# Pooled attention and a top-1 expert layer in one kernel: one two-bank buffer for an attention product, and its division in single VectorE instructions

## The chip, the cores and the metric

The kernel runs on one core of a Trainium2 chip. The core has TensorE (PE in the profile, its weight loads PEld), VectorE (DVE), ScalarE (ACT), GpSimd (POOL) and a queue of DMA issues on SyncE (SP). The metric is the device time of one execution in microseconds; of several runs the median counts.

## The reference

Attention over keys and values that are averaged in groups of 8 rows, then a layer of 8 experts, of which each token takes the one with the largest gate logit. Batch 8, 8 heads, 576 positions, head width 64; so 4608 tokens of width 512, and experts of 512 x 1024 and 1024 x 512.

```python
def _attn_ref(q, k, v):
    k_p = k.reshape(B, H, Sp, pool, D).mean(axis=3)
    v_p = v.reshape(B, H, Sp, pool, D).mean(axis=3)
    scores = scale * np.matmul(q, k_p.transpose(0, 1, 3, 2))
    scores = scores - np.max(scores, axis=-1, keepdims=True)
    attn = np.exp(scores)
    attn = attn / (np.sum(attn, axis=-1, keepdims=True) + 1e-09)
    return np.matmul(attn, v_p).astype(np.float32)

def _moe_ref(x, modality_id, w_gate, modality_bias, w1, w2):
    logits = x @ w_gate + modality_bias[modality_id]
    e_idx = np.argmax(logits, axis=1)
    probs = softmax(logits)
    gate_w = probs[np.arange(N), e_idx]
    for e in range(E):
        mask = e_idx == e
        h = np.maximum(x[mask] @ w1[e], 0.0)
        out[mask] = gate_w[mask, None] * (h @ w2[e])
```

The softmax of the gate is shortened here; the attention's output, transposed to one row per token, is x.

## The kernel before

The order of all instructions on all engines is the order in which the program writes them; buffers come from pools, and a recording layer adds the waits. A wait is put where an instruction touches a buffer that another engine wrote or read, so which bytes count as one buffer decides who waits for whom.

**Attention.** The 4608 tokens are 36 tiles of 128. Two tiles, or one tile of two half-filled sequences ("mixed"), make a step; there are 20 steps, and the loop over n (lines 874 to 947) writes parts of three neighbouring steps between each other. For a tile the scores of all heads go through max, subtraction and exp (s_dve, s_act), are turned (t_pe, t_act), and multiplied by the averaged values (a_pe). Each head's values carry 73 columns: 64 values, 8 products with the gate's weights, and a 1 whose product is the softmax's sum. Eight heads times 73 columns need two PSUM banks of 512 columns: bank u holds heads 4u to 4u+3. In a_pe each bank is a tile of its own, av0 and av1, with one buffer each; three groups of matmuls fill each (lines 570 and 574, two of 570 and one of 574).

x_dve (lines 576 to 608) divides. For each of the two banks VectorE takes the four sums (L593), their reciprocals (L595), then writes the values into xb (L597) and the gate's products into lg (L599). Between them gap(1) lets one instruction out of a list of small fillers, `drip`: the routing of the tiles already done. These are the softmax over the gate's logits, the counts of tokens by expert (cum, L684) and the early table of slots. Some fillers are held until TensorE has a place for them. When four or five tiles are complete, their rows go to xs in DRAM (L607, SyncE).

GpSimd averages keys and values meanwhile (fold, L294 to L296), and splits the first expert's weights (split_lo, L139) into a rounded part and a rest.

**Expert layer.** Slots of 256 tokens with one expert each; 19 slots are run. A slot has eight blocks f of 128 hidden columns. `first` (lines 159 to 168) makes 12 matmuls into hp[f % 2], ScalarE writes the rounded hidden values hh (L165), VectorE the rest hlo (L167); `second` makes six matmuls of hh and hlo into op (L1100). They alternate: block f+1's first layer stands before block f's second layer, so that hh and hlo have time.

```python
hp = [ps_av.tile([P, 512], F32, tag=f"av{i}", name=f"hp{i}") for i in range(2)]
...
first(f, a, b, hp[f % 2][:, 0:SLOT], *(at or (hhs[f % 2], hlos[f % 2])))()
```

hp0 and hp1 take the banks of av0 and av1 over. The number of slots is known only at run time; the last slot's second half (`end`, lines 1158 to 1169) stands in a branch and orders the second layer differently: between two blocks stand three matmuls for one half of the tokens, and the other half's follow at the end.

Of the kernel before, what the change touches and what calls it, by code (L numbers as in the profile page):

```python
# [9 lines left out]
F32 = mybir.dt.float32  # L10
# [5 lines left out]
ALU = mybir.AluOpType  # L16
# [6 lines left out]
P = 128  # L23
# [7 lines left out]
def kernel(  # L31
# [12 lines left out]
    nc = tc.nc  # L44
    ctx.enter_context(tc.manual_schedule(engines=ENGINES))
    B, H, S, HD = q.shape
    NTOK, D = out.shape
    E, _, FF = w1.shape
    POOL = 8
# [3 lines left out]
    VC = HD + E + 1  # L53
# [15 lines left out]
    ps_av = ctx.enter_context(tc.tile_pool(name="ps_av", bufs=1, space=PSUM))  # L69
# [114 lines left out]
    with ExitStack() as actx:  # L184
        ap = actx.enter_context(tc.tile_pool(name="ap", bufs=1))
# [270 lines left out]
        def gap(n=2):  # L456

            for _ in range(n):
                if drip and drip[0] not in held:
                    drip.pop(0)()  # L460
# [7 lines left out]
        qts, pqs, scs, pes, pps, pts, avs, xb, lgs = {}, {}, {}, {}, {}, {}, {}, {}, {}  # L468
# [87 lines left out]
        def a_pe(t):  # L556
            n, z = tile_step[t]
            b, jj, _ = steps[n]
            pt, pt4 = pts.pop(t), pt4z[z]
            av = [ps_av.tile([P, 512], F32, tag=f"av{u}", name=f"av_{t}_{u}") for u in range(2)]  # L560
            avs[t] = av
            if jj is not None:
                halves = [(slice(0, P), b % NB)]
            else:
                halves = [(slice(64 * y, 64 * y + 64), (b - 1 + y) % NB) for y in range(2)]
            for u in range(2):
                for gg in range(2):
                    c = 2 * u + gg
                    for hs, y in halves:
                        nc.tensor.matmul(av[u][hs, 2 * VC * gg:2 * VC * (gg + 1)], pt[:, c, hs],  # L570
                                         vw[y][:, c].rearrange("p a x -> p (a x)"), start=(gg == 0), stop=False)
                dst4 = av[u][:, 0:4 * VC].rearrange("p (g x) -> p g x", g=2)[:, :, VC:2 * VC]
                for hs, y in halves:
                    nc.tensor.matmul(dst4[hs], pt4[:, hs], v4[y][:, 2 * u:2 * u + 2, :], start=False, stop=True)  # L574

        def x_dve(t):
            n, z = tile_step[t]
            g, gi = tile_group[t]
            av = avs.pop(t)
# [6 lines left out]
            if gi == 0:  # L586
                lgs[g] = ap.tile([P, GT, H, E], F32, tag="lg", bufs=2, name=f"lg_{g}")
            xo = xb[b, 4] if mixed else xb[b][:, gi % 5, :]
            for u in range(2):
                avv = av[u][:, 0:4 * VC].rearrange("p (h x) -> p h x", h=4)  # L590
                r = ap.tile([P, 4], F32, tag="r", bufs=4, name=f"r_{t}_{u}")
                rb = r.rearrange("p (h o) -> p h o", o=1)
                nc.vector.tensor_scalar(r, avv[:, :, VC - 1], float(POOL), 1e-9 * POOL, op0=ALU.mult, op1=ALU.add)  # L593
                gap(1)
                nc.vector.reciprocal(r, r)  # L595
                gap(1)
                nc.vector.tensor_tensor(xo[:, u * D // 2:(u + 1) * D // 2].rearrange("p (h d) -> p h d", h=4), avv[:, :, 0:HD],  # L597
                                        rb.to_broadcast([P, 4, HD]), op=ALU.mult)
                nc.vector.tensor_tensor(lgs[g][:, gi, 4 * u:4 * u + 4, :], avv[:, :, HD:HD + E],  # L599
                                        rb.to_broadcast([P, 4, E]), op=ALU.mult)  # L600

            if mixed:
                for z in range(2):
# [355 lines left out]
    xl.append(mp.tile([P, ND, SLOT], F32R, name="xl1"))  # L959
    ps_op = ctx.enter_context(tc.tile_pool(name="ps_op", bufs=1, space=PSUM))  # L960
    op = [[ps_op.tile([P, 512], F32, name=f"op{i}_{z}") for z in range(2)] for i in range(2)]
    hp = [ps_av.tile([P, 512], F32, tag=f"av{i}", name=f"hp{i}") for i in range(2)]
    hhs = [mp.tile([P, SLOT], F32R, name=f"hh{i}") for i in range(2)]
    hlos = [mp.tile([P, SLOT], F32R, name=f"hlo{i}") for i in range(2)]

# [263 lines left out]
```

## Time and profile before

| | us |
|---|---|
| median of 3 runs (662.88 to 668.61) | 663.94 |
| the profiled execution | 669.24 |
| its span, first to last instruction | 667.4 |

The profile is one execution, taken by the hardware profiler; times in its rows are from the span's start. "L597" is line 597 of the kernel, and `xb<-av,r` says that xb is written from av and r. "x72" counts instructions; a mean in ns belongs to one of them. A row of the waits names who waited, for whom, the sum in us, how often and the longest. A row of the timeline has start and duration in us, and in brackets how long the engine stood before and what released it. Matmuls are pipelined: they begin every 0.1 to 0.3 us, though each lasts some 0.3 to 0.4 in the rows.

Attention ends at about 210 us, the expert loop runs from about 222 to 640, and the last slot ends the kernel.

### The profile page before, as it was taken

The numbers are of one execution on the slowest core, as the hardware profiler recorded it, in microseconds if no ns is written. First come the engines' busy times: TensorE is split into PE (matmuls) and PEld (weight loads), VectorE is DVE, ScalarE is ACT, GpSimd is POOL, SyncE is SP. The second block draws the span as 40 slices with busy tenths as digits, with TensorE's granted clock in tenths as the row PEclk, the third lists the DMA queues.
The fourth block names the chain that finished last, engine by engine and source line by source line (L and its number), as shares of the span: only waits on it lengthen the run. The fifth ranks groups of instructions, "written<-read, shape, count | busy, mean of one in ns | idle before, by whom it ended". The sixth has DMA issues, their size and how long they took to land.

```text
span 667.4 us, 12673 instructions
## 1 busy us (share of the span) xinstructions
PE 613.7 (92%) x4313; PEld 556.7 (83%) x4313; DVE 433.9 (65%) x955; ACT 340.9 (51%) x625; POOL 211.6 (32%) x236
## 2 busy tenths in 40 slices
PE   4399899998599799999999999999999999999993
PEld 3289788887498699999999999999999999999982
DVE  4677789899975656766655656665565666556540
ACT  2347556676351254544555555555555555555530
POOL 5388673955801022112112112211211321131221
PEclk9799899999799899999999999999999999999998
DMA  9999999998232372011011055101105510110120
GB/s 244 223 363 241 316 155 232 274 172 243 53 80 64 87 230 64 18 48 64 12 54 63 20 179 182 50 17 61 63 18 178 186 38 16 63 65 17 48 69 15
DMA packets 65403, 76.54 MB, mean 115 GB/s; under 512 B 15407, under 2 KB 42031, under 8 KB 65328
## 3 DMA queue, kind: packets, MB, share of 16 engines
q1 hardware_dynamic: 59088, 55.68, 32.1%
q0 software_dynamic: 6240, 19.95, 9.0%
q8 instruction: 36, 0.59, 0.4%
q14 instruction: 39, 0.32, 0.2%
HBM read 119.64 MB, written 19.42 MB: 208 GB/s over the span
## 4 chain that ended last, share of the span: by engine, by line
PE 67%; DMA 17%; DVE 4%; SPq 4%; issue 3%; POOL 2%; ACT 1%; POOLq 0%; DVEq 0%; ACTq 0%
PE hp L163 27%; PE op L1100 26%; DMA out_dram<-ob,sidx 7%; DMA v<-in_v_dram 5%; PE av L570 3%; PE xt L154 2%; DMA q<-in_q_dram 2%; PE ph L163 2%; DMA xs<-xb 2%; DMA k<-in_k_dram 1%; PE av L574 1%; DVE sm L672 1%; PE pp L535 1%; PE sc L506 1%; PE ptab L1006 1%
## 5 line engine op out<-in xcount | busy, mean ns | idle before, releaser
L136 ACT CAST hl<-raw 128x1024 fp32r<-128x1024 f32 x138 | 145.0, 1051 | 143.8 <-PE op L1100 141.8
L163 PE MATMUL hp<-xh,hl 128*128 128x256 f32 x1152 | 186.0, 284 | 0.6 <-issue 0.6
L163 PEld LDWEIGHTS hp<-xh,hl 128*128 128x128 f32 x1152 | 166.1, 189 | 11.7 <-issue 1.0
L1100 PE MATMUL op<-hl,hh 128*128 128x512 f32 x556 | 174.2, 394 | 0.0
L1086 POOL DMA_INDIRECT out_dram<-ob,sidx x38 | 53.7, 1413 | 353.3 <-DVE ob L1082 268.4
L139 DVE TENSOR_TENSOR hl<-raw,hl 128x1024 fp32r<-128x1024 f32 x136 | 165.3, 1216 | 0.0
L167 DVE SCALAR_TENSOR_TENSOR hlo<-hp,hh 128x256 fp32r<-128x256 f32 x139 | 58.9, 424 | 140.5 <-ACT hh L165 129.7
L1100 PE MATMUL op<-hl,hlo 128*128 128x512 f32 x278 | 108.9, 392 | 0.0
L1100 PEld LDWEIGHTS op<-hl,hh 128*128 128x128 f32 x556 | 95.2, 189 | 12.3
L163 PE MATMUL hp<-xl,hl 128*128 128x256 f32 x576 | 92.0, 282 | 0.0
L163 PEld LDWEIGHTS hp<-xl,hl 128*128 128x128 f32 x576 | 78.9, 190 | 0.0
L165 ACT ACTIVATE hh<-hp 128x256 fp32r<-128x256 f32 x139 | 53.3, 383 | 49.3 <-PE hp L163 47.4
L1100 PEld LDWEIGHTS op<-hl,hlo 128*128 128x128 f32 x278 | 52.2, 188 | 11.8
L570 PE MATMUL av<-vw,pt 128*128 128x146 f32 (+1 forms) x320 | 52.1, 303 | 9.3 <-DVE lg L599 8.4
L570 PEld LDWEIGHTS av<-vw,pt 128*128 128x128 f32 (+1 forms) x320 | 41.3, 187 | 11.5 <-DVE lg L599 9.1
L143 POOL DMA_INDIRECT xg<-xs,gidx x40 | 42.9, 1074 | 12.1 <-issue 9.5
L506 PE MATMUL sc<-kt,qt 128*128 128x144 f32 x256 | 38.2, 293 | 0.8 <-DVE sb L516 0.6
L513 DVE TENSOR_REDUCE mx<-sc 128x8 f32<-128x576 f32 (+1 forms) x40 | 27.7, 693 | 16.2 <-ACT pt L554 10.6
L540 ACT COPY pt<-pp 128x512 f32<-128x512 f32 x36 | 21.1, 586 | 31.2 <-PE pp L535 31.0
L294 POOL TENSOR_TENSOR v<-v 128x256 f32<-128x256 f32 (+2 forms) x16 | 23.6, 1473 | 38.5 <-DMA v<-in_v_dram 38.5
L157 DVE TENSOR_TENSOR xl<-xt,xh 128x512 fp32r<-128x512 f32 x38 | 24.7, 686 | 16.9 <-ACT xh L156 16.8
L506 PEld LDWEIGHTS sc<-kt,qt 128*128 128x128 f32 x256 | 34.1, 195 | 1.6 <-PE pp L535 1.4
(226 smaller groups left out, 756.5 us busy)
## 6 DMA issues: line engine op xcount, KB each, us to landing
raw<-in_moe_w_dram SPq DMA_DIRECT2D x304, 256.0 KB
xs<-xb SPq DMA_DIRECT2D x8, 1024.0 KB
k<-in_k_dram SPq DMA_DIRECT2D x7, 1024.0 KB
v<-in_v_dram SPq DMA_DIRECT2D x7, 1024.0 KB
q<-in_q_dram SPq DMA_DIRECT2D x6, 1024.0 KB
q<-in_q_dram SPq DMA_DIRECT2D x4, 512.0 KB
v<-in_v_dram SPq DMA_DIRECT2D x16, 128.0 KB
k<-in_k_dram SPq DMA_DIRECT2D x4, 256.0 KB
```

What stands on the lines that cost most here:

```text
L136: nc.scalar.copy(hl[f][:, 0, :], raw[f])
L139: eng.tensor_sub(hl[f][:, 1, :], raw[f], hl[f][:, 0, :].bitcast(F32))
L143: nc.gpsimd.indirect_dma_start(out=xgs[(2 * s + tt) % len(xgs)], out_offset=None, in_=xs[0:rows, :], in_offset=IndirectOffsetOnAxis(idx[:, ...
L157: nc.vector.tensor_sub(b[:, :, sl], pt, a[:, :, sl].bitcast(F32))
L163: nc.tensor.matmul(ph, hl[f][:, w, d * P:(d + 1) * P], x[:, d, :], start=(n == 0 and d == 0), stop=(n == 2 and d == ND - 1))
L165: nc.scalar.activation(hh, ph, AF.Relu)
L167: nc.vector.scalar_tensor_tensor(hlo, ph, 0.0, hh.bitcast(F32), op0=ALU.max, op1=ALU.subtract)
L506: nc.tensor.matmul(dst, qt[:, i, :], kt[b % NB][:, :, h * SPL:(h + 1) * SPL], start=True, stop=True)
L513: nc.vector.reduce_max(mx, scv, axis=AX.X)
L570: nc.tensor.matmul(av[u][hs, 2 * VC * gg:2 * VC * (gg + 1)], pt[:, c, hs], vw[y][:, c].rearrange("p a x -> p (a x)"), start=(gg == 0), sto ...
L1086: nc.gpsimd.indirect_dma_start(out=out[:, :], out_offset=IndirectOffsetOnAxis(idx.bitcast(U32), 0), in_=ob, in_offset=None, bounds_check=N ...
L1100: nc.tensor.matmul(o[tt], l[:, ts_], hl[f][:, w, D:2 * D], start=(f == 0 and n == 0), stop=(f == NF - 1 and n == 2))
```

## The change

Three places. In a_pe the two tiles av0 and av1 become one tile av of [128, 2, 512], with one buffer; the matmuls are the same, in the same order. In x_dve the loop over the two banks goes: each of the four divisions' instructions now covers both banks, and gap(2) stands where gap(1) stood twice. In the expert layer hp0 and hp1 become views of one tile of the same shape, since the banks now have one name.

```diff
-            av = [ps_av.tile([P, 512], F32, tag=f"av{u}", name=f"av_{t}_{u}") for u in range(2)]
+            av = ps_av.tile([P, 2, 512], F32, tag="av", name=f"av_{t}")
...
-            for u in range(2):
-                avv = av[u][:, 0:4 * VC].rearrange("p (h x) -> p h x", h=4)
-                r = ap.tile([P, 4], F32, tag="r", bufs=4, name=f"r_{t}_{u}")
-                rb = r.rearrange("p (h o) -> p h o", o=1)
-                nc.vector.tensor_scalar(r, avv[:, :, VC - 1], float(POOL), 1e-9 * POOL, op0=ALU.mult, op1=ALU.add)
-                gap(1)
-                nc.vector.reciprocal(r, r)
-                gap(1)
-                nc.vector.tensor_tensor(xo[:, u * D // 2:(u + 1) * D // 2].rearrange("p (h d) -> p h d", h=4), avv[:, :, 0:HD],
-                                        rb.to_broadcast([P, 4, HD]), op=ALU.mult)
-                nc.vector.tensor_tensor(lgs[g][:, gi, 4 * u:4 * u + 4, :], avv[:, :, HD:HD + E],
-                                        rb.to_broadcast([P, 4, E]), op=ALU.mult)
+            avv = av[:, :, 0:4 * VC].rearrange("p u (h x) -> p u h x", h=4)
+            r = ap.tile([P, 2, 4], F32, tag="r", bufs=4, name=f"r_{t}")
+            rb = r.rearrange("p u (h o) -> p u h o", o=1)
+            nc.vector.tensor_scalar(r, avv[:, :, :, VC - 1], float(POOL), 1e-9 * POOL, op0=ALU.mult, op1=ALU.add)
+            gap(2)
+            nc.vector.reciprocal(r, r)
+            gap(2)
+            nc.vector.tensor_tensor(xo.rearrange("p (u h d) -> p u h d", u=2, h=4), avv[:, :, :, 0:HD],
+                                    rb.to_broadcast([P, 2, 4, HD]), op=ALU.mult)
+            nc.vector.tensor_tensor(lgs[g][:, gi].rearrange("p (u h) e -> p u h e", u=2), avv[:, :, :, HD:HD + E],
+                                    rb.to_broadcast([P, 2, 4, E]), op=ALU.mult)
...
-    hp = [ps_av.tile([P, 512], F32, tag=f"av{i}", name=f"hp{i}") for i in range(2)]
+    hp2 = ps_av.tile([P, 2, 512], F32, tag="av", name="hp")
+    hp = [hp2[:, i, :] for i in range(2)]
```

In the changed program the lines behind the first of these places carry numbers that are one lower (L592 is L593 of before).

VectorE's order at tile 28, in step 15, before: the tile's two banks (r_28_0 and r_28_1), from behind its first instruction L593 on, with the fillers L655, L656, L657 and L671 of the routing in between, and the filler L672 behind.

```order
L655 SCALAR_TENSOR_TENSOR lgr_2_2196<-lgr_2_2196,w8_163 128x72 [waits Activation_49]
L595 RECIPROCAL r_28_0_2347<-r_28_0_2347 128x4 [waits DVE_49]
L656 TENSOR_REDUCE m2_2_2199<-lgr_2_2196 128x9 [waits DVE_49]
L597 TENSOR_TENSOR xb_6_2281<-av_28_0_2339,r_28_0_2347 128x256 [waits DVE_49]
L599 TENSOR_TENSOR lg_3_2282<-av_28_0_2339,r_28_0_2347 128x32
L593 TENSOR_SCALAR r_28_1_2354<-av_28_1_2340 128x4 [waits PE_49]
L657 TENSOR_TENSOR oh_90<-w8_163,m2_2_2199 128x72 [waits DVE_49]
L595 RECIPROCAL r_28_1_2354<-r_28_1_2354 128x4 [waits DVE_49]
L671 TENSOR_REDUCE sm_2_2200<-ex_2_2197 128x9
L597 TENSOR_TENSOR xb_6_2281<-av_28_1_2340,r_28_1_2354 128x256 [waits DVE_49]
L599 TENSOR_TENSOR lg_3_2282<-av_28_1_2340,r_28_1_2354 128x32
L672 TENSOR_SCALAR sm_2_2200<-sm_2_2200 128x9 [waits DVE_49]
```

The same place in the changed program, from the tile's first instruction on; L671 here is L672 of before.

```order
L592 TENSOR_SCALAR r_28_2178<-av_28_2171 128x8 [waits PE_49]
L654 SCALAR_TENSOR_TENSOR lgr_2_2034<-lgr_2_2034,w8_163 128x72 [waits Activation_49]
L655 TENSOR_REDUCE m2_2_2037<-lgr_2_2034 128x9 [waits DVE_49]
L594 RECIPROCAL r_28_2178<-r_28_2178 128x8
L656 TENSOR_TENSOR oh_90<-w8_163,m2_2_2037 128x72 [waits DVE_49]
L670 TENSOR_REDUCE sm_2_2038<-ex_2_2035 128x9
L596 TENSOR_TENSOR xb_6_2118<-av_28_2171,r_28_2178 128x512 [waits DVE_49]
L598 TENSOR_TENSOR lg_3_2119<-av_28_2171,r_28_2178 128x64
L671 TENSOR_SCALAR sm_2_2038<-sm_2_2038 128x9 [waits DVE_49]
L672 TENSOR_REDUCE dc_2_2039<-oh_90 128x8
L513 TENSOR_REDUCE mx_17_1_2225<-sc_17_1_2201 128x2x2 [waits PE_49,Activation_49]
L675 RECIPROCAL gate_92<-sm_2_2038 128x9 [waits DVE_49]
```

Four instructions of the division stand where eight stood, the fillers come two by two, and all of them ahead of the values' division; L672 of before still follows the tile. The first instruction waits for TensorE once, for the last matmul of both banks.

TensorE's order in the expert loop, slot 1, block 7 and the first block of the next slot, before. In brackets stand the engines that a matmul waits for.

```order
L163 MATMUL hp1_2863<-xh1_2853,hl7_2636 128x256 x4
L1100 MATMUL op1_0_2860<-hl6_2390,hh0_2864 128x512 [waits Activation_49]
L1100 MATMUL op1_0_2860<-hl6_2390,hh0_2864 128x512
L1100 MATMUL op1_0_2860<-hl6_2390,hlo0_2866 128x512 [waits DVE_49]
L1100 MATMUL op1_1_2861<-hl6_2390,hh0_2864 128x512 x2
L1100 MATMUL op1_1_2861<-hl6_2390,hlo0_2866 128x512
L163 MATMUL hp0_2862<-xh0_87,hl0_1740 128x256 [waits Activation_49]
L163 MATMUL hp0_2862<-xh0_87,hl0_1740 128x256 x3
```

The same place in the changed program: the end of block 7, the second layer of block 6, and the next block's start.

```order
L163 MATMUL hp_2646<-xh1_2637,hl7_2444 128x256 x4
L1100 MATMUL op1_0_2644<-hl6_2216,hh0_2647 128x512 [waits Activation_49]
L1100 MATMUL op1_0_2644<-hl6_2216,hh0_2647 128x512
L1100 MATMUL op1_0_2644<-hl6_2216,hlo0_2649 128x512
L1100 MATMUL op1_1_2645<-hl6_2216,hh0_2647 128x512 x2
L1100 MATMUL op1_1_2645<-hl6_2216,hlo0_2649 128x512
L163 MATMUL hp_2646<-xh0_87,hl0_1620 128x256 [waits DVE_49]
L163 MATMUL hp_2646<-xh0_87,hl0_1620 128x256 x3
```

The wait for VectorE has moved from the second layer's hlo matmul to the first matmul of the next block; what it waits for there is L167 of the block before, which reads the other bank. The second layer still waits for hh of ScalarE.

TensorE's order in the last slot's branch, where three second-layer matmuls stand between two blocks, before:

```order
L1100 MATMUL op1_0_2860<-hl4_2104,hx1_1_2899 128x512 [waits DVE_49]
L163 MATMUL hp0_2862<-xh1_2853,hl6_2390 128x256 x4
L163 MATMUL hp0_2862<-xl1_2854,hl6_2390 128x256 x4
L163 MATMUL hp0_2862<-xh1_2853,hl6_2390 128x256 x4
L1100 MATMUL op1_0_2860<-hl5_2254,hx2_0_2900 128x512 [waits Activation_49]
L1100 MATMUL op1_0_2860<-hl5_2254,hx2_0_2900 128x512
L1100 MATMUL op1_0_2860<-hl5_2254,hx2_1_2901 128x512 [waits DVE_49]
```

And in the changed program:

```order
L1100 MATMUL op1_0_2644<-hl4_1954,hx1_1_2682 128x512
L163 MATMUL hp_2646<-xh1_2637,hl6_2216 128x256 [waits DVE_49]
L163 MATMUL hp_2646<-xh1_2637,hl6_2216 128x256 x3
L163 MATMUL hp_2646<-xl1_2638,hl6_2216 128x256 x4
L163 MATMUL hp_2646<-xh1_2637,hl6_2216 128x256 x4
L1100 MATMUL op1_0_2644<-hl5_2092,hx2_0_2683 128x512 [waits Activation_49]
L1100 MATMUL op1_0_2644<-hl5_2092,hx2_0_2683 128x512
```

Here too each block's first matmul now waits for VectorE's L167 of the block before, with three matmuls between them.

More of the change, by code (lines that the diff above doesn't have):

```diff
@@ L569, in a_pe @@
                     for hs, y in halves:
-                        nc.tensor.matmul(av[u][hs, 2 * VC * gg:2 * VC * (gg + 1)], pt[:, c, hs],
+                        nc.tensor.matmul(av[hs, u, 2 * VC * gg:2 * VC * (gg + 1)], pt[:, c, hs],
                                          vw[y][:, c].rearrange("p a x -> p (a x)"), start=(gg == 0), stop=False)
-                dst4 = av[u][:, 0:4 * VC].rearrange("p (g x) -> p g x", g=2)[:, :, VC:2 * VC]
+                dst4 = av[:, u, 0:4 * VC].rearrange("p (g x) -> p g x", g=2)[:, :, VC:2 * VC]
                 for hs, y in halves:
```

## The prediction

> **What bounds the kernel now.** First the page: its head, the engines' shares and the slices.
>
> ```profile
> span 667.4 us, 12673 instructions
> PE 613.7 (92%) x4313; PEld 556.7 (83%) x4313; DVE 433.9 (65%) x955; ACT 340.9 (51%) x625; POOL 211.6 (32%) x236
> ...
> PE   4399899998599799999999999999999999999993
> ...
> DMA  9999999998232372011011055101105510110120
> ```
>
> A slice is 16.7 us. TensorE (PE) is full nearly everywhere; the DMA engines are full as long as the attention loads run. The windows view, attention in the first row, the expert loop in the second:
>
> ```profile
> 33.00:210.00 177.00, 158.47 (x1307) 146.03 (x1308) 148.85 (x509) 102.37 (x262) 105.36 (x115) 0.96 0.81 202
> ...
> 222.00:640.00 418.00, 418.00 (x2798) 380.70 (x2797) 258.71 (x393) 223.90 (x330) 87.47 (x70) 1.00 0.23 74
> ```
>
> The columns are PE, weight loads, VectorE (DVE), ScalarE (ACT), GpSimd (POOL), clock, DMA. Attention is the only stage in which VectorE (148.9 of 177 us) comes near TensorE (158.5). So I read next what TensorE waits for there, from the view of the waits between 33 and 215 us (sum, times, longest):
>
> ```profile
> PE av L570 <- DVE lg L599: 8.4, 2, 7.8
> ...
> PE pv L361 <- POOL vp L296: 5.5, 3, 3.1
> PE sc L500 <- DVE sb L516: 1.2, 1, 1.2
> PE av L570 <- DVE r L593: 0.7, 1, 0.7
> PE sc L506 <- DVE sb L516: 0.6, 1, 0.6
> PE sc L376 <- DVE sb L516: 0.6, 2, 0.4
> ```
>
> VectorE ends 11.5 us of waits, 7.8 of them in a single one. That one, in the timeline:
>
> ```profile
> 169.10 9.31 DVE L672 TENSOR_SCALAR sm<-sm 128x9 f32<-128x9 f32 x1
> ...
> 179.00 0.10 DVE L684 TENSOR_TENSOR cum<-cum,dc 128x8 bf16<-128x8 bf16 x1
> ...
> 180.13 0.18 DVE L599 TENSOR_TENSOR lg<-av,r 128x32 f32<-128x32 f32 x1
> ...
> 169.13 9.25 POOL L139 TENSOR_TENSOR hl<-raw,hl 128x1024 fp32r<-128x1024 f32 x4
> ...
> 180.37 1.34 PE L570 MATMUL av<-vw,pt 128*128 128x146 f32 x4 [7.75 <-DVE lg L599]
> ```
>
> A nine-column instruction stands for 9.31 us and ends 0.03 us after the last of four GpSimd subtractions. It is not VectorE's amount of work that makes this wait.
>
> **The division itself.** The groups by line:
>
> ```profile
> L597 DVE TENSOR_TENSOR xb<-av,r 128x256 f32<-128x256 f32 x72 | 30.4, 422 | 1.7
> L157 DVE TENSOR_TENSOR xl<-xt,xh 128x512 fp32r<-128x512 f32 x38 | 24.7, 686 | 16.9 <-ACT xh L156 16.8
> L1082 DVE TENSOR_SCALAR ob<-op,xg 128x512 f32<-128x512 f32 x19 | 14.1, 743 | 0.9 <-PE op L1100 0.6 <-DVE hlo L167 0.3
> L599 DVE TENSOR_TENSOR lg<-av,r 128x32 f32<-128x32 f32 x72 | 13.0, 180 | 0.0
> L595 DVE RECIPROCAL r<-r 128x4 f32<-128x4 f32 x72 | 12.6, 176 | 1.6
> L593 DVE TENSOR_SCALAR r<-av 128x4 f32<-128x4 f32 x72 | 11.0, 152 | 10.0 <-PE av L574 9.8
> ```
>
> A tile now costs 2 x (152 + 176 + 422 + 180) = 1860 ns. From 32 to 256 columns the time grows by 242 ns in 224, 1.08 ns a column. So 512 columns take 422 + 277 = 700 ns, between the 686 and 743 of the two rows of that width; 64 columns take 215; the two small ones barely grow (156 and 180). That is 1251 ns, 0.61 us less a tile, 22 us over 36 tiles. What of it reaches the end is decided by the waits. Leaving out the 7.8, VectorE ends 11.5 - 7.8 = 3.7 us of TensorE's waits. Against that stand two delays. The new first instruction must see all six groups of the product, where the old one began after three; and the next product must wait for the whole tile, 0.16 + 0.18 + 0.70 + 0.22 = 1.25 us after the start instead of 0.93 for the first bank. Where VectorE works without a gap the saving wins; where it keeps up, a product can come some 0.3 us later. Part of a gain is also taken back at the POOL wait (5.5 us), whose end hangs on loads. Ends: -3.7 us and +0.7 (two such delays). I take **-1.5**, nearer to the middle, since only some of the waits lie behind the last load.
>
> **The long wait.** The tile ahead of L672 is 0.6 us shorter, so L672 comes at about 168.5, before 169.13, and escapes. But the addition to cum (L684) stands four rows behind it; from the end of L672 at 178.41 to cum at 179.00 the rows between take 0.6. With 0.1 for L672 itself cum comes at 168.5 + 0.7 = 169.2, just after the GpSimd work has begun, and it is of the same kind:
>
> ```profile
> 83.39 2.35 DVE L684 TENSOR_TENSOR cum<-cum,dc 128x8 bf16<-128x8 bf16 x1
> ```
>
> So the stand moves from the one to the other and still ends at about 178.4. The rows between, 0.6 us, are then done before it, and the tile behind it frees its banks 0.3 later: **-0.3**.
>
> [...]
>
> **End of attention.** The last tile is divided before the last store. Its product, and VectorE on the second half:
>
> ```profile
> 208.98 0.41 PE L574 MATMUL av<-vw,pt 128*128 128x146 f32 x2
> ...
> 209.59 0.15 DVE L593 TENSOR_SCALAR r<-av 128x4 f32<-128x4 f32 x1
> ...
> 209.99 0.42 DVE L597 TENSOR_TENSOR xb<-av,r 128x256 f32<-128x256 f32 x1
> ```
>
> It ends at 210.41. The new chain cannot begin before 209.39; 0.40 later (209.59 to 209.99) comes xb, and 0.70 after that it ends, at 210.49. **+0.1**: the half that ran beside the product no longer does.
>
> **The expert loop.** hp0 and hp1 become views of one buffer. By the order of the changed program the first matmul of every hidden block waits for VectorE's L167 of the block before, though that reads the other bank. Between two blocks stand six second-layer matmuls. An ordinary pair and the one after the output's scaling (19 slots, row L1082):
>
> ```profile
> 397.04 0.42 DVE L167 SCALAR_TENSOR_TENSOR hlo<-hp,hh 128x256 fp32r<-128x256 f32 x1 [1.22 <-ACT hh L165]
> ...
> 402.79 0.42 DVE L167 SCALAR_TENSOR_TENSOR hlo<-hp,hh 128x256 fp32r<-128x256 f32 x1 [0.70 <-ACT hh L165]
> ...
> 397.59 0.66 PEld L163 LDWEIGHTS hp<-xh,hl 128*128 128x128 f32 x4
> ...
> 403.22 0.66 PEld L163 LDWEIGHTS hp<-xh,hl 128*128 128x128 f32 x4
> ```
>
> L167 ends at 397.46, 0.13 us before the weight load that is to wait for it; TensorE starts 0.06 after a VectorE end (180.31 to 180.37 above). That fits, so it costs nothing: the six matmuls cover it, by 0.07 us. After the scaling it is 403.21 to 403.22, 0.05 too late; the load runs ahead of its matmul, so between 0 and 0.05 x 18 = 0.9 us. I take **+0.3**, nearer to zero because that lead is longer than 0.05. The first block of slot 1 is late for a different reason, VectorE's tables:
>
> ```profile
> 229.08 0.42 DVE L167 SCALAR_TENSOR_TENSOR hlo<-hp,hh 128x256 fp32r<-128x256 f32 x1
> ...
> 229.15 0.52 PE L163 MATMUL hp<-xh,hl 128*128 128x256 f32 x3
> ```
>
> It may start at 229.50 + 0.06 and not at 229.15: **+0.4**.
>
> **The last slot** has only three matmuls between blocks, and ACT comes late after the branch:
>
> ```profile
> 644.76 0.39 ACT L165 ACTIVATE hx<-hp 128x256 fp32r<-128x256 f32 x1 [3.01 <-issue]
> 645.83 0.38 ACT L165 ACTIVATE hx<-hp 128x256 fp32r<-128x256 f32 x1 [0.68 <-PE hp L163]
> ...
> 645.25 0.42 DVE L167 SCALAR_TENSOR_TENSOR hx<-hp,hx 128x256 fp32r<-128x256 f32 x1 [3.96 <-ACT hx L165]
> ...
> 644.19 0.66 PE L163 MATMUL hp<-xh,hl 128*128 128x256 f32 x4
> ...
> 646.33 0.63 PE L163 MATMUL hp<-xh,hl 128*128 128x256 f32 x4
> ```
>
> Block 4 starts at 644.19; it must now wait for 645.67 + 0.06: +1.54. From a block's start to its ACT is 1.64, to VectorE 0.41 more, its length 0.42, the release 0.06: 2.53 where blocks now follow each other in 2.13. Three more blocks add 3 x 0.4. **+2.7**, all on the path, since the last output is behind it.
>
> Sum: -1.5 - 0.3 + 0.1 + 0.3 + 0.4 + 2.7 = +1.7 us. The profiled execution took 669.24 us (span 667.4), 5.3 above the median of 663.94; by it 670.9, against the median 665.6.
>
> **The rivals.** (1) The long wait goes: cum also comes before 169.13, or it passes at the end of the first GpSimd subtraction, 169.13 + 9.25/4 = 171.4, instead of at 178.4. Then 6.9 us fall away: 658.7, and less than 657.3 if the -3.7 comes in place of the -1.5. For it speaks that cum arrives within 0.1 us of the edge; against it, that L672 did not pass at any of three such ends. [...] (2) Every wait in the expert loop costs: if TensorE needs more than the 0.13 us between the end of L167 and the weight load, each of 18 x 7 pairs without transposes between pays the excess; at 0.20 it is 0.07 x 126 = 8.8 us, 674.4. Against it speaks the 0.06 of the one row; for it, that this row shows a TensorE that stood idle. It decides from 0.13 on. (3) The shorter division changes nothing that TensorE sees, because loads and matmuls set the pace: without the -1.5 and the -0.3 it is 667.4.
>
> **How the numbers follow.** Forecast 0.42, rival 1 0.32, rival 2 0.10, rival 3 0.16. One per cent, about what a measurement of this kernel tells from no change, reaches from 657.3 to 670.6. Below lies the third of rival 1 that also has the larger gain, 0.11; above lie rival 2 and a little of rival 3, 0.12; between them 0.77. The range from 657.5 to 669.5 leaves these out and holds the bounds of the terms.
>
> **What would show it.** Right: the division's four lines at about 1.25 us a tile, 45 us in all; no TENSOR_SCALAR of 9 us, but a cum of about 9; blocks of the last slot 2.5 us apart; a block and its six matmuls in the loop as now, (403.22 - 397.59) / 2 = 2.8 us. Wrong: waits of TensorE for hlo in ordinary blocks (rival 2), no stand at 169 us (rival 1), TensorE's waits for VectorE unchanged in sum (rival 3).

## The result, and the profile after

| | median of all executions | ratio to before | 95% interval |
|---|---|---|---|
| before (4 executions) | 664.83 us (662.88 to 668.61) | 1 | |
| changed (4 executions) | 675.58 us (674.99 to 677.16) | 1.0145 | 1.0103 to 1.0186 |

The change makes the kernel slower by 1.45%, 9.6 us by the ratio and 10.75 by the medians. Forecast were 665.6 us and a range up to 669.5. The profiled execution of the changed kernel took 675.57 us (span 673.9), which is its median; that of before took 669.24, 4.4 above its own. So the two profiles stand 6.5 us apart, less than the kernels do. Single executions of one kernel scatter by 10 us here, and the ratios below leave out those more than 1.5% above a kernel's fastest, while the medians beside them take in all.

The head and two slices of the page of the changed kernel:

```profile
span 673.9 us, 12518 instructions
PE 618.8 (92%) x4313; PEld 559.9 (83%) x4313; DVE 426.2 (63%) x811; ACT 340.9 (51%) x625; POOL 210.8 (31%) x236
...
PE   4499799797599899999999999999999999999983
...
PEclk9799999799889899999999999999999999999998
```

VectorE has 144 instructions less and 7.7 us less busy time (433.9 to 426.2). TensorE's work is the same 4313 matmuls. The two pages' slices differ most ahead of slice 14, in attention; the 3 us that the last slot loses (below) are too few to show in a slice of some 17 us. The windows view of the two stages, with the columns of before:

```profile
33.00:210.00 177.00, 154.81 (x1264) 143.16 (x1263) 138.34 (x357) 100.41 (x258) 103.53 (x115) 0.93 0.79 198
222.00:640.00 418.00, 416.19 (x2780) 378.23 (x2781) 258.01 (x397) 222.46 (x328) 86.05 (x69) 1.00 0.23 74
```

In attention both engines are less busy: TensorE 154.8 us where it was 158.5, VectorE 138.3 where it was 148.9, and the granted clock is 0.93 where it was 0.96. Less is done in the same 177 us, 1264 matmuls and not 1307. Both engines wait more, which points to waits for each other. TensorE's waits between 33 and 215 us, and VectorE's for the product between 33 and 216:

```profile
PE av L570 <- DVE lg L598: 18.8, 8, 6.9
PE pv L361 <- POOL vp L296: 1.5, 1, 1.5
PE sc L376 <- DVE sb L516: 0.5, 1, 0.5
```

```profile
DVE r L592 <- PE av L574: 19.9, 16, 8.8
```

A product now waits for the division of the tile before it eight times, 18.8 us in all (twice and 8.4 before), and the division waits for a product sixteen times, 19.9 us (five times and 9.8). Without the longest wait of each, this row sums to 11.9 us where it summed to 0.6. The durations of the division's own four lines came out as forecast:

```profile
L596 DVE TENSOR_TENSOR xb<-av,r 128x512 f32<-128x512 f32 x36 | 24.8, 690 | 0.9
L598 DVE TENSOR_TENSOR lg<-av,r 128x64 f32<-128x64 f32 x36 | 7.7, 215 | 0.0
L594 DVE RECIPROCAL r<-r 128x8 f32<-128x8 f32 x36 | 7.2, 199 | 0.8
L592 DVE TENSOR_SCALAR r<-av 128x8 f32<-128x8 f32 x36 | 5.8, 162 | 20.2 <-PE av L574 19.9
```

That is 690 + 215 + 199 + 162 = 1266 ns a tile against 1860, 21.4 us less over 36 tiles. But VectorE's busy time fell by 7.7 us only, and most of the reason is in the rows: an instruction on VectorE begins before the row of the one ahead of it has ended (a row of 0.69 us from 83.96, shown further down, is followed at 84.57). From one start to the next, without a wait between, the four lines take 930 ns a tile by the medians of the changed trace (608 + 130 + 119 + 73) and took 1206 (twice 341 + 98 + 95 + 69). So the saving is 0.28 us a tile, 9.9 us over 36, and not the 0.61 and 22 that a sum of durations gives.

The long stand, in the timeline:

```profile
172.50 9.27 DVE L671 TENSOR_SCALAR sm<-sm 128x9 f32<-128x9 f32 x1
...
172.47 9.26 POOL L139 TENSOR_TENSOR hl<-raw,hl 128x1024 fp32r<-128x1024 f32 x4
...
184.04 1.34 PE L570 MATMUL av<-vw,pt 128*128 128x146 f32 x4 [6.93 <-DVE lg L598]
```

The same nine-column instruction still stands: it and the GpSimd work both come some 3.4 us later than before, and meet again. In the last slot, the starts of blocks 3 to 7 (the first matmuls of each):

```profile
644.77 0.71 PE L163 MATMUL hp<-xh,hl 128*128 128x256 f32 x4 [0.76 <-DVE hl L139]
...
649.03 0.74 PE L163 MATMUL hp<-xh,hl 128*128 128x256 f32 x4 [1.20 <-DVE hx L167]
...
651.66 0.73 PE L163 MATMUL hp<-xh,hl 128*128 128x256 f32 x4 [0.23 <-DVE hx L167]
...
654.30 0.74 PE L163 MATMUL hp<-xh,hl 128*128 128x256 f32 x4 [0.24 <-DVE hx L167]
...
656.93 0.74 PE L163 MATMUL hp<-xh,hl 128*128 128x256 f32 x4 [0.23 <-DVE hx L167]
```

Blocks follow each other in 2.63 us, where it was 2.13.

One column of the windows view was shown ahead of the result and not used: the clock. Stretches of 3.41 us around two of the waits of the changed kernel; the first number behind the comma is TensorE's busy time, the third from the end the clock:

```profile
80.23:83.65 3.42, 0.85 (x8) 0.64 (x7) 3.39 (x5) 1.53 (x6) 3.34 (x2) 1.00 1.04 348
83.65:87.06 3.41, 3.41 (x15) 3.40 (x16) 0.84 (x4) 0.00 (x0) 3.17 (x6) 0.50 1.24 226
87.06:90.47 3.41, 3.41 (x31) 3.41 (x30) 2.58 (x6) 1.64 (x4) 1.88 (x2) 1.00 1.38 58
...
175.81:179.22 3.41, 1.30 (x12) 1.06 (x10) 3.41 (x1) 0.13 (x1) 3.41 (x2) 1.00 0.01 2
179.22:182.63 3.41, 0.00 (x0) 0.00 (x0) 3.41 (x6) 0.00 (x0) 2.52 (x2) 0.50 0.00 0
182.63:186.05 3.42, 2.01 (x8) 2.01 (x9) 3.31 (x8) 2.01 (x5) 1.59 (x1) 0.50 0.17 1
186.05:189.46 3.41, 3.41 (x17) 3.40 (x16) 1.81 (x5) 0.92 (x2) 0.75 (x1) 0.50 0.00 0
```

After a stretch in which TensorE worked 0.85 us, the next runs at half speed: 15 matmuls where the one after it holds 31. A wait of 2.6 us has so cost about another 1.7, half of the 3.41 us worked at half speed. This became a theory of its own below.

### The profile page after: what moved, and what is told of

The parts are those of the page before. It is cut to its first block, busy times and chain, and to the rows that moved or that the text cites. A ratio compares the mean times of both kernels' runs of the same rounds, so it can differ in the third digit from the quotient of the medians.

```text
span 673.9 us, 12518 instructions
## 1 busy us (share of the span) xinstructions
PE 618.8 (92%) x4313; PEld 559.9 (83%) x4313; DVE 426.2 (63%) x811; ACT 340.9 (51%) x625; POOL 210.8 (31%) x236
## 4 chain that ended last, share of the span: by engine, by line
PE 68%; DMA 11%; DVE 9%; issue 5%; SPq 3%; ACT 2%; POOL 0%; POOLq 0%; ACTq 0%; DVEq 0%
PE hp L163 26%; PE op L1100 25%; DMA out_dram<-ob,sidx 7%; PE av L570 4%; PE xt L154 2%; PE sc L506 2%; PE av L574 2%; DMA q<-in_q_dram 2%; PE ph L163 2%; PE pp L535 1%; DMA xs<-xb 1%; DVE mx L513 1%; PE ptab L1006 1%; DVE xb L596 1%; DVE arow L698 1%
## 5 line engine op out<-in xcount | busy, mean ns | idle before, releaser
L1086 POOL DMA_INDIRECT out_dram<-ob,sidx x38 | 52.3, 1377 | 355.5 <-DVE ob L1082 274.7
L167 DVE SCALAR_TENSOR_TENSOR hlo<-hp,hh 128x256 fp32r<-128x256 f32 x139 | 58.9, 424 | 141.2 <-ACT hh L165 130.3
L570 PE MATMUL av<-vw,pt 128*128 128x146 f32 (+1 forms) x320 | 53.7, 310 | 19.3 <-DVE lg L598 18.8
L570 PEld LDWEIGHTS av<-vw,pt 128*128 128x128 f32 (+1 forms) x320 | 43.2, 193 | 22.0 <-DVE lg L598 16.8
L574 PE MATMUL av<-vw,pt 128*128 128x146 f32 (+1 forms) x160 | 32.1, 305 | 0.4 <-ACT pt L554 0.3
```

The source lines that it names most:

```text
L167: nc.vector.scalar_tensor_tensor(hlo, ph, 0.0, hh.bitcast(F32), op0=ALU.max, op1=ALU.subtract)
L570: nc.tensor.matmul(av[hs, u, 2 * VC * gg:2 * VC * (gg + 1)], pt[:, c, hs], vw[y][:, c].rearrange("p a x -> p (a x)"), start=(gg == 0), sto ...
L1086: nc.gpsimd.indirect_dma_start(out=out[:, :], out_offset=IndirectOffsetOnAxis(idx.bitcast(U32), 0), in_=ob, in_offset=None, bounds_check=N ...
```

## The experiments

All runs in one table; 1 is the kernel before on the same chip.

| run | what it is | median us | before | ratio | 95% interval |
|---|---|---|---|---|---|
| base | before, again | 668.29 | 665.3 | 0.9999 | 0.9954 to 1.0044 |
| hp_split | changed, expert buffers apart | 671.72 | 665.3 | 1.0090 | 1.0056 to 1.0124 |
| hp_only | before, expert buffers one | 671.23 | 665.3 | 1.0062 | 1.0017 to 1.0107 |
| one_buffer | one product buffer, old halves | 678.13 | 665.3 | 1.0204 | 1.0143 to 1.0264 |
| gaps_late | hp_split, fillers behind the division | 672.70 | 666.39 | 0.9994 | 0.9927 to 1.0062 |
| b_gaps_late | before, fillers behind the division | 676.07 | 666.39 | 1.0126 | 1.0085 to 1.0167 |
| spread | gaps_late, GpSimd's work spread | 672.88 | 666.39 | 1.0103 | 1.0071 to 1.0134 |
| late_start | before, division starts late | 668.04 | 666.22 | 1.0064 | 1.0026 to 1.0102 |
| late_release | before, first bank comes free late | 673.04 | 666.22 | 1.0118 | 1.0064 to 1.0171 |
| b_split0 | before, ScalarE's copies spread | 663.98 | 666.22 | 0.9961 | 0.9919 to 1.0002 |
| b_mix | before, less GpSimd work at 170 us | 660.71 | 667.78 | 0.9881 | 0.9841 to 0.9921 |
| gate_probe | before, copies at eight places (one execution) | 679.79 | 666.39 | | |

### Which part costs: base, hp_split, hp_only, one_buffer

**The kernel before, a second time.**

> The kernel before, unchanged, profiled a second time. Every theory: 664.8 +- 1.5 us, ratio 1.000. What it tells is whether the profile on which the forecast rested was an ordinary one: if it was, the nine-column instruction of line 672 stands some 9 us again and attention's last division ends at about 210 us. If not, the stand is shorter or gone and the end lies some 4 us earlier, at about 206.

Its time did not differ, and a stand of 9 us was there again, but another filler had it, L657 in the middle of a division and not L672 behind one:

```profile
169.14 9.42 DVE L657 TENSOR_TENSOR oh<-w,m 128x72 bf16<-128x72 f32 x1
```

Attention ended at 213.5 us, later than in the first profile (210.4), not earlier. In the profile of hp_only below, whose attention is that of before, it ended at 205.2 (that execution, 663.30 us, was the fastest of its ten), and in that of gate_probe at 206.6. So four profiles of the same attention lie 8 us apart. In that of base TensorE stood 2.9 us for the scores at 123 us, and the clock was half for two stretches behind it (columns as above):

```profile
118.95:122.37 3.42, 1.07 (x10) 0.83 (x8) 3.42 (x6) 0.59 (x1) 3.26 (x3) 1.00 1.09 167
122.37:125.78 3.41, 2.83 (x16) 2.48 (x17) 3.12 (x17) 1.33 (x5) 3.25 (x5) 0.50 1.06 250
125.78:129.19 3.41, 3.41 (x16) 3.40 (x16) 1.96 (x9) 0.86 (x2) 1.64 (x2) 0.50 0.75 90
```

In hp_only neither the wait nor the low clock is there.

**The changed kernel with the expert loop's buffers apart.** Attention's product banks get a pool that ends with attention, and the two hidden-layer buffers are two tiles of a pool of their own:

```diff
...
-    hp2 = ps_av.tile([P, 2, 512], F32, tag="av", name="hp")
-    hp = [hp2[:, i, :] for i in range(2)]
+    hp = [ps_hp.tile([P, 512], F32, name=f"hp{i}") for i in range(2)]
```

> The changed kernel, with the two hidden-layer buffers of the expert loop separate again (attention as changed). Theory A (the expert loop costs what was forecast, 3.8 us, and the rest, about 7 us, is lost in attention): 675.6 - 3.8 = 671.8 us. Theory B (the expert loop's common buffer costs all of it, attention gains nothing or little): 665 us or less.

671.72 us, and by the ratio 6.0 us above before (0.0090 x 665.3; 3.7 to 8.2 by the interval). Theory A's number.

**The kernel before with only those two made one.**

The pools are those of hp_split.

```diff
...
-    hp = [ps_av.tile([P, 512], F32, tag=f"av{i}", name=f"hp{i}") for i in range(2)]
+    hp2 = ps_hp.tile([P, 2, 512], F32, name="hp")
+    hp = [hp2[:, i, :] for i in range(2)]
```

> The kernel before, with only the two hidden-layer buffers of the expert loop made one (attention as before). Theory A: 664.8 + 3.8 = 668.6 us, with the blocks of the last slot 2.5 us apart. Theory B: 675 us.

By the ratio 4.1 us above before (1.1 to 7.1), against 3.8 by theory A. In its profile the last slot's blocks are 2.63 us apart. 6.0 and 4.1 make 10.1; the whole change is 9.6. So the two parts add up within their intervals, and the one that went against the forecast is attention: 6.0 us lost where 1.7 were to be gained. The move to other pools, which both runs have, was not run alone.

**One product buffer, but the old halves** (with the expert buffers apart; the edit against the changed kernel):

```diff
-            avv = av[:, :, 0:4 * VC].rearrange("p u (h x) -> p u h x", h=4)
...
+            for u in range(2):
+                avv = av[:, u, 0:4 * VC].rearrange("p (h x) -> p h x", h=4)
...
```

> Attention's two product banks are one buffer, but the division is written in halves as before, with its fillers between; the expert loop's buffers stay separate. Theory A1 (what costs in attention is the place of the fillers: all stand now ahead of the division of the values, and one that is held up by GpSimd delays both banks): the halves keep the old order, so 664.8 to 666.5 us. Theory A2 (the buffer itself costs: the next product must wait until both banks are divided, however that is written): 671 us or more, since the division is also long again.

13.6 us above before by the ratio: theory A1 falls, A2 holds. In the order of this kernel the first instruction of a tile's division waits for the last matmul of the product though it reads only the first bank, and the first matmul of a product waits for the last instruction of the division before it: the dependency is by tile. In the waits between 33 and 222 us of TensorE:

```profile
PE av L570 <- DVE sm L672: 10.0, 1, 10.0
PE av L570 <- DVE lg L599: 9.1, 7, 3.6
```

So the common buffer costs 13.6 us (9.5 to 17.5 by the interval). The rest of the change in attention, the merged instructions and the fillers' new places together, wins back 13.6 - 6.0 = 7.6 of them by the ratios and 6.4 by the medians (678.13 and 671.72).

### Is it the fillers: gaps_late, b_gaps_late

The three waits of hp_split for a product that were long, besides the one at 184 us, all lay behind a filler that stood for GpSimd in the middle of a division. The first, in hp_split's timeline:

```profile
81.11 2.70 DVE L683 TENSOR_TENSOR cum<-cum,dc 128x8 bf16<-128x8 bf16 x1
83.74 0.19 DVE L594 RECIPROCAL r<-r 128x8 f32<-128x8 f32 x1
83.96 0.69 DVE L596 TENSOR_TENSOR xb<-av,r 128x512 f32<-128x512 f32 x1
84.57 0.21 DVE L598 TENSOR_TENSOR lg<-av,r 128x64 f32<-128x64 f32 x1
...
81.45 2.34 POOL L294 TENSOR_TENSOR v<-v 128x1024 f32<-128x1024 f32 x1
...
84.93 0.82 PE L570 MATMUL av<-vw,pt 128*128 128x146 f32 x2 [2.55 <-DVE lg L598]
```

The addition to cum stands until GpSimd's addition ends at 83.79, and both banks with it. So the fillers were moved behind the division, in the changed kernel with expert buffers apart and in the kernel before:

```diff
-            gap(2)
             nc.vector.reciprocal(r, r)
-            gap(2)
...
+            gap(4)
```

> The changed kernel with the expert loop's buffers separate (671.7 us) and the four fillers of a tile all placed behind the division instead of two and two ahead of the values. Theory F (the waits of TensorE at 84.9, 125.1 and 161.5 us, 2.7 + 3.9 + 3.8 us, come from fillers that stand for GpSimd between the first and the last instruction of the division, and hold both banks; two of them also halve the clock for one or two stretches of 3.4 us): these three go, some 10 us of waits less what comes back as later stands of the scores' instructions, so 661 to 666 us. Theory R (the stands only move: the maximum of the scores is late by the same amount, and TensorE waits there): 670 us or more.

> The kernel before, with the fillers between the instructions of each half placed behind both halves instead. Theory F: here, too, the first bank comes free without a filler ahead of it; the waits at 81.8 and 122.9 us shrink and fewer runs lie at the upper end of the spread: 660 to 664 us. Theory R: 665 us or more, and no ordering of the fillers explains the changed kernel.

Theory F's number came in neither kernel, but for two executions. In the profile of gaps_late the long waits for the product went, except the one at 183 us:

```profile
PE av L570 <- DVE lg L596: 9.8, 5, 8.9
PE sc L500 <- DVE sb L516: 3.9, 2, 3.3
PE sc L756 <- DVE b L766: 1.8, 1, 1.8
```

In their place TensorE waits 3.9 us for the scores' instructions and 1.8 for the table. Two of its twelve executions took 662.4 and 662.7 us, the other ten 670.2 to 680.4, so that the ratio says nothing certain; the median of all, 6.3 us above that of before, is as far from it as hp_split's 6.4. Why two came out 8 us lower stays open. In the kernel before the same move costs 8.4 us by the ratio, and there theory F falls. A filler's stand is paid for wherever the next thing that TensorE wants lies behind it; of the orders run with two buffers, the old one, between the instructions of each half, is the cheaper.

### Late start or late release: late_start, late_release

The common buffer adds two waits. Each can be had alone with two banks. For the late start the second half's sum is scaled first, so that the division begins after all six groups; for the late release the two banks of odd tiles change places in the product and in the division, so that the next product begins in the bank that was divided last:

```diff
+            for u in (1, 0):
+                nc.vector.tensor_scalar(rs[u], avvs[u][:, :, VC - 1], float(POOL), 1e-9 * POOL, op0=ALU.mult, op1=ALU.add)
             for u in range(2):
...
```

```diff
-            for u in range(2):
+            for u in ((0, 1) if t % 2 == 0 else (1, 0)):
```

> The kernel before (two banks apart, halves, fillers as they were), but the second half's sum is scaled first, so that VectorE starts on a tile only after all six matmul groups of its product; the first bank still comes free ahead of the second half. It tells apart the two waits that the common buffer adds (14 us together, from the kernel with one buffer and the old halves). Theory S (the late start costs: VectorE stands idle behind the product, 20 us in all where it stood 2 to 10): 671 to 677 us, and VectorE's waits for the product at 15 us or more. Theory Q (the late release costs: TensorE stands until both banks are divided): 664 to 668 us.

> The kernel before, with the banks of odd tiles taken in the other order by the product and by the division alike: a division still starts after three groups, but the next product begins in the bank that was divided last, and so waits for the whole division. Theory S: 664 to 668 us. Theory Q: 671 to 677 us, with TensorE's waits for the division at 15 us or more.

Both cost: 4.3 us for the late start (1.7 to 6.8), 7.9 for the late release (4.3 to 11.4), together 12.2 against the 13.6 of the common buffer; each of these has an interval of 5 to 8 us. Theory Q's numbers are met by late_release (673.04 us, 12.4 + 10.0 us of waits), theory S's by neither in full: late_start has the 15.3 us of VectorE's waits that it named, but only a part of the time. TensorE's waits between 33 and 222 us in late_release:

```profile
PE av L570 <- DVE lg L599: 12.4, 8, 3.5
PE av L570 <- DVE sm L672: 10.0, 1, 10.0
```

The waits of more than 1 us lie at 80, 85, 124 and 161 us, and at 183; in the changed kernel they lie at 84, 124, 160 and 184. What the two have in common is the late release. Without the long one, TensorE's waits of this kind sum to 12.4 us in late_release and 11.9 in the changed kernel; in the four profiles with the old order they sum to between nothing and 4.6. VectorE waits for the product longer in late_start (15.3 us) than in late_release (10.9), at about half the cost by the middle values; as the two intervals overlap, it is likely and not certain that TensorE's waits for the bank are the dearer ones.

### What a wait costs besides its length: gate_probe

```diff
...
+            for _ in range({4: 5, 5: 6, 6: 7, 7: 8, 8: 9, 9: 10, 10: 12, 11: 16}.get(s, 0) if f == 2 else 0):
+                nc.vector.tensor_copy(scratch, iota_f[:, 0:1].to_broadcast([P, 512]))
             rest()
```

> The kernel before, with copies that nothing uses on VectorE ahead of one block's low half (block 2 of slots 4 to 11: 5, 6, 7, 8, 9, 10, 12 and 16 copies of 128x512), so that TensorE has to wait at eight places of the otherwise full expert loop, longer from one to the next. Theory G (TensorE's granted clock falls to half for one or more stretches of 3.41 us when it has stood for some 2 us or more, so such a wait costs its own length and up to 1.7 us for each stretch besides): no low clock at the shortest waits, one at each of the longest, and a time of the slot that grows by more than the wait there. Rival (the low clock in attention has another cause, the loads or the mixed work there): the clock stays at 1.00 at all eight, and each slot grows by its wait alone.

The copies made no wait of TensorE in slots 5 and 6, and waits of 0.28, 0.68, 1.21, 2.15 and 3.98 us in slots 7 to 11. Against the kernel before, the block starts move by 0.55, 0.97, 1.50, 2.44 and 6.41 us: 0.3 more than the wait at the first four, 2.4 more at the last. The stretches around the last two:

```profile
457.46:460.87 3.41, 1.80 (x11) 1.62 (x12) 3.34 (x7) 0.57 (x1) 0.42 (x1) 1.00 0.42 134
460.87:464.28 3.41, 3.41 (x25) 3.17 (x25) 2.30 (x3) 1.92 (x3) 0.00 (x0) 1.00 0.00 0
...
481.35:484.76 3.41, 1.42 (x10) 0.99 (x9) 3.17 (x8) 0.99 (x2) 2.06 (x2) 1.00 0.55 167
484.76:488.17 3.41, 1.42 (x3) 1.17 (x4) 3.31 (x8) 0.00 (x0) 0.00 (x0) 0.50 0.18 64
488.17:491.59 3.42, 3.42 (x15) 3.22 (x14) 1.12 (x1) 1.21 (x2) 0.00 (x0) 0.50 0.00 0
```

A wait of 2.15 us left TensorE 1.80 of 3.41 us busy in its stretch, and the clock stayed. The one of 3.98 fell across two stretches of 1.42 each, and both of the following ran at half speed; half of the 1.42 + 3.42 us worked there is 2.42, which is the excess. So theory G is right that a long wait is paid twice, in this one execution and for the wait of 3.98 us, but the length of a wait did not decide alone: in slot 4 a stretch at half speed followed a wait of only 1.11 us, ahead of 36 matmuls of 28 columns, and none followed the one of 2.15. How busy TensorE was in a stretch of 3.41 us, 1.80 at the wait of 2.15 and twice 1.42 at that of 3.98, tells more; the counts over all profiles stand in the last section.

### Can the long stand be shortened: spread, b_split0, b_mix

**spread** starts the eight subtractions of the experts' weights over seven steps, two of them in step 17 and one in each of the others, on top of gaps_late:

```diff
-        for f, n in enumerate((15, 15, 16, 16, 17, 17, 18, 19)):
+        for f, n in enumerate((13, 14, 15, 16, 17, 17, 18, 19)):
```

> As the kernel with the fillers behind the division, and the GpSimd subtractions of the experts' weights go to one step each (steps 13 to 19) instead of two in each of the steps 15 to 17. If the 9 us stand is the sum of four subtractions that follow each other without a gap, it falls to 4.7 us, TensorE's wait there from 7 to some 2.5 us, and the low clock behind it from 6.8 or 10.2 us to 3.4 or none: 4.5 to 7 us less than the kernel with the fillers behind the division alone. If one subtraction would hold VectorE as long for another reason (the data that it waits for), no change.

It missed. Three subtractions still followed each other (177.9 to 184.9 us) and a filler stood for 7.7; TensorE waited 2 to 3 us at 75, 85 and 153 us, and seven stretches of attention ran at half speed (four in gaps_late).

**b_split0** moves ScalarE's copies, for which the subtractions wait, in the kernel before:

```diff
-        for f, n in enumerate((12, 13, 14, 15, 15, 16, 17, 19)):
+        for f, n in enumerate((12, 13, 14, 15, 16, 17, 18, 19)):
```

> The kernel before, with ScalarE's copies of the experts' weights, for which the GpSimd subtractions wait, one step apart from the fourth on (steps 12 to 19, one each, instead of two in step 15). If that keeps the subtractions from following each other without a gap, the stand of 9 us at 170 us falls to 4.7 or less, and with it some 4.6 us of waiting and one or two stretches of low clock: 657 to 662 us. If they bunch all the same, or another instruction stands there as long, 663 to 667 us.

They bunched all the same: three subtractions in a row instead of four, a stand of 7.1 us, and 2.6 us less by the ratio, which the interval does not quite tell from none.

**b_mix** has the copies of b_split0 and takes three of the subtractions away from GpSimd besides:

```diff
...
-        for f, n in enumerate((15, 15, 16, 16, 17, 17, 18, 19)):
-            at(hook_3, n, lambda f=f: split_lo(f, nc.gpsimd))
+        for f, n in enumerate((15, 15, 16, 17, 17, 18, 18, 19)):
+            at(hook_3, n, lambda f=f: split_lo(f, nc.vector if f in (3, 4, 5) else nc.gpsimd))
```

> The kernel before, with ScalarE's copies of the experts' weights one step apart, and three of the eight subtractions (blocks 3, 4 and 5, steps 17 to 18) on VectorE instead of GpSimd, where they take 1.22 us each as in the expert loop. If what VectorE stands for at 170 us is the run of GpSimd subtractions, only one or two are left there: the stand falls from 9 us to 2.4 or 4.7, TensorE's wait from 8 to 2 or 4, its low clock there to one stretch or none; against that 3.7 us more work on VectorE in steps that have it idle 2 to 4 us each: 657 to 661 us. If another stand takes its place, or VectorE has not the room, 664 us or more.

It is faster than both kernels: 0.9881 of before (0.9841 to 0.9921), 7.9 us. What is left of the stand and of the wait, in the timeline:

```profile
163.88 2.67 DVE L657 TENSOR_TENSOR oh<-w,m 128x72 bf16<-128x72 f32 x1
...
167.35 0.89 PE L570 MATMUL av<-vw,pt 128*128 128x146 f32 x3 [2.32 <-DVE sm L672]
```

The stand is 2.7 us long and the wait 2.3, both as expected. So a gain in attention lay in what VectorE stood for; fewer instructions to divide with, bought with a common buffer, had brought none.

## Why the prediction was wrong

**What bounds the kernel: right in the place, incomplete in the price.** VectorE and the long wait in attention were what mattered; b_mix shows what that wait is worth. But the clock column, 0.96 in the quoted row of attention, was left out of every price. In the changed kernel TensorE works 12.6 us of attention in six stretches at half speed, 6.3 us lost. An account of attention from the traces, from the end of the first tile's division to that of the last, in us (idle is time without a matmul in the rows; the loss is half of the work at half speed):

| profile | time | TensorE idle | lost at half speed | rest |
|---|---|---|---|---|
| before | 173.0 | 18.2 | 3.1 | 151.6 |
| base | 178.4 | 19.3 | 5.3 | 153.8 |
| hp_only | 169.5 | 16.7 | 1.4 | 151.3 |
| gate_probe | 171.8 | 17.5 | 2.9 | 151.4 |
| changed | 179.5 | 22.1 | 6.3 | 151.1 |
| hp_split | 179.4 | 21.9 | 6.3 | 151.3 |
| b_mix | 166.3 | 11.5 | 3.4 | 151.4 |

The first four have the attention of before, the next two the changed one, and the last has the shorter stand. The rest is the same to 0.5 us in all but base, so TensorE's waits and its low clock account for the loss; from the mean of the first four to that of the next two the waits grow by 4.1 us and the loss at half speed by 3.1.

**The division itself: the step that failed.** The durations were right (1251 ns forecast, 1266 measured), but "0.61 us less a tile" adds up rows that overlap; the engine gained 0.28. Wrong above all was "a product can come some 0.3 us later", and so the end "+0.7 (two such delays)" and the -1.5 between. The common buffer with the old halves costs 13.6 us, not 0.7, and the merged instructions with the fillers' new places win back some 7 (7.6 by the ratios, 6.4 by the medians), where 3.7 was the bound of the gain. The forecast priced the later release by the division's busy time alone, 1.25 against 0.93 us. What lies ahead of the release is longer: up to four fillers, where two stood ahead of the first bank's, and their stands (2.7, 2.9 and 1.8 us at the three places in hp_split), and behind the wait the half clock. And it happens at eight products, not two. The late release alone costs 7.9 us and the late start 4.3, by the middle values. That the place of the fillers alone is to blame is not so: moved behind the division in the kernel before, they were paid for at the scores.

**The long wait: wrong in the mechanism, small in the number.** Forecast was that L672 comes ahead of GpSimd's work and escapes, and that cum stands instead, -0.3. It did not escape (L671 in the changed kernel, 9.27 us), since the tiles ahead were 3.4 us later, as was GpSimd's work. TensorE's wait was 6.9 us instead of 7.8. Nor could the forecast have held from one execution to the next: in two more profiles of the same attention, base and hp_only, L657 stood there, for 9.42 and 9.55 us. So it is luck which filler meets the subtractions, and the working to 0.1 us rested on one profile. Rival 1, with a chance of 0.32, fell with it; its other way, a pass at the end of the first subtraction, did not come either, as L671 stood over all four (9.27 us over 9.26).

**End of attention: right.** From the last matmul's end to the last value it took 1.17 us (214.30 to 215.47) where it had been 1.02, +0.15 against +0.1. What followed was not foreseen: the time from the last store's issue to the counts, 10.6 us, shrank to 8.0, so that of the 5.1 us by which attention ended later in the profile 2.6 were left at the first block of the expert loop.

**The expert loop and the last slot: right in the last slot, untested in the loop.** From the profiles, slot 1 lost 0.34 us (0.4 forecast), the loop up to block 138 0.36 (0.3), and from there to the end 3.1 (2.7): block 4 came 1.3 later (1.54), each of the next three 0.5 (0.4). Together 3.8 against 3.4, and 4.1 in the run with this part alone. The last slot and slot 1 lose by the waits that were named. The loop's 0.36 shows nothing: base, without any change, took 0.9 us longer than the first profile over the same blocks. Rival 2, ordinary blocks that wait, did not come. Rival 3 had no saving in attention and a total of 667.4; it had no loss either.

**The range.** Above it lay only rival 2 and a little of rival 3. No rival had attention lose, though the quoted row of the division's first line, with 9.8 us of waits for the product (7.8 of them in one), showed that VectorE waits for TensorE as well as TensorE for VectorE.

## What to carry to other kernels

Merging two buffers into one to merge the instructions on them made each side wait for all of the other here, 13.6 us with the old halves: price the start and the release over everything that lies between them in the consumer's queue, fillers and their stands included, and not by the instructions that were merged. Price the saving from start to start, where rows of an engine overlap (0.28 us a tile here, not 0.61). A wait of the engine that sets the pace cost about its length here (0.28 to 2.15 us of wait and 0.3 more) and, where it left a stretch of 3.41 us no more than 42% busy, up to half of the next stretch or stretches besides (2.4 us behind the wait of 3.98). When an engine's instructions stand for as long as another engine works, moving that work can pay more than making the held engine's own work shorter: here it gained 7.9 us, and some 10 us less work on VectorE, had at the price of a common buffer, ended in a loss.

## What the runs showed of the hardware

**The changes of the clock lie on a grid.** In each of 14 profiled executions all changes of TensorE's granted clock lie a whole number of 3.413 us apart, and the low stretches ahead of the last matmul are 3.41, 6.83 or 10.24 us long. Between 30 and 640 us, with the clock full: of 39 stretches with TensorE up to 42% busy all were followed by one at half speed; of 5 between 43 and 46% one; of 21 between 47 and 59% none; of 30 between 60 and 70% five, of which the one in gate_probe lies over matmuls of 28 columns; of 2312 above that none. Of the stretches at half speed, 62 were 83% busy or more, and 59 of these were followed by a full one; of the 33 others, up to 74%, none.

**A small VectorE instruction stood for as long as GpSimd's subtractions went on.** A filler stood 9.3 us over four subtractions of 2.3 us each (before and changed), 7.7 over three (spread), 7.1 over three (b_split0), 2.7 over one (b_mix), and ended 0.03 to 0.1 us after the last of them. In none of these did it end between two subtractions that followed each other without a gap. In another place of before one did: over two subtractions from 158.53 to 163.21 us, L734 stood from 159.83 to 160.92, about the end of the first, and L735 from there to 163.24. Why the one passed and the others did not was not shown.

**Rows of VectorE overlap.** The medians from one start to the next, without a wait between, are 0.08 to 0.09 us shorter than the division's rows: 341 ns against 422 for 256 columns, 608 against 690 for 512. Two instructions made one have so saved about 0.07 us, not 0.15 (2 x 422 - 690).

**The scatter of before has a cause that can be seen.** Its attention ended at 205.2, 206.6, 210.4 and 213.5 us in four profiles, and the account above puts most of the differences down to TensorE's waits and to 1.4 to 5.3 us lost at half speed. A wait of 2.15 us in gate_probe left its stretch 1.80 us busy and the clock stayed; one of 2.57 in the changed kernel left its stretch 0.85 us busy and the next ran at half speed. An estimate from these two and the counts above is that for a wait of 2 to 3 us it depends on how it lies in the grid, so that a small shift of everything may move the time by some microseconds either way. That this makes up the whole of the scatter was not tried.
